# Loading all spectral weights of an attention and Fourier mixing kernel by casting GpSimd DMAs

## The chip, the cores and the metric

The kernel runs on one core of a Trainium2 chip. A core has a matrix engine (PE, with a separate weight load, PEld), a vector engine (DVE), a scalar engine (ACT), GpSimd (POOL) and a queue engine (SP), which work side by side and wait for each other through semaphores. Sixteen DMA engines move data between HBM and the on-chip memory (SBUF). A DMA is issued by an engine's instruction stream, here by SP or by POOL, and it is issued only when the instructions before it in that stream have been issued. PE writes its sums to a second memory, PSUM. The metric is the device time of one execution in microseconds (us); lower is better.

## The reference

Sliding-window attention with a linear distance bias is followed by a mixing layer in the Fourier domain, for 8 sequences of 576 tokens and a width of 512 (8 heads of 64):

```python
def _attn_ref(q, k, v):
    window, scale = 128, 1.0 / np.sqrt(D)
    scores = scale * np.matmul(q, k.transpose(0, 1, 3, 2))
    scores = np.where(mask, scores + bias[None], -1000000000.0)
...
    return np.matmul(attn, v).astype(np.float32)

def _moe_ref(x, w_r, w_i, w_ch):          # 64 modes, each with 512 x 512 matrices w_r and w_i
    X = np.fft.rfft(x, axis=1)
    Xr, Xi = (np.real(X[:, :n_modes]), np.imag(X[:, :n_modes]))
    Yr = np.einsum('bmd,mde->bme', Xr, w_r) - np.einsum('bmd,mde->bme', Xi, w_i)
    Yi = np.einsum('bmd,mde->bme', Xr, w_i) + np.einsum('bmd,mde->bme', Xi, w_r)
    Y[:, :n_modes] = Yr + 1j * Yi
    y = np.fft.irfft(Y, n=S, axis=1)
    u = x + y
    return (u + np.maximum(u @ w_ch, 0.0)).astype(np.float32)
```

All inputs are fp32. Each of the 128 matrices w_r[m] and w_i[m] is 1 MB, and each is used once. The imaginary matrix of mode 0 adds nothing that the output keeps, so the kernel loads 127 of them: 133 MB of the 162.5 MB that it reads.

## The kernel before

**Attention (0 to 138 us).** The work is cut into 16 units of one sequence and four heads. A hand-written table, STAGE, says which step of which unit runs in which stage: scores on PE, exp on ACT, mask and normalisation on DVE, values on PE. SP loads q, k and v in fp32 into the tiles qr, kr and vr. After two units of a sequence PE takes its Fourier transform, and the spectrum goes into the tile XC.

**Weight tiles.** A weight tile holds one matrix, 128 partitions by 4 times 512 elements. `load_w` (L450) issues its load in one of two ways:

- As bf16 (L458 to L460): a GpSimd DMA reads the fp32 matrix and casts it on the way into a tile of 4 KB a partition. During attention one such tile is loaded in each of the stages named in AHEAD, after a small copy on POOL (L533) that waits for a finished piece of x. These 14 tiles make up the pool `early` (EARLY). Seven more go into the `spare` tiles, which are the memory of qr, kr and vr after its last use (LATER). Eight later loads, the list `again` (L545), go into `early` a second time.
- As fp32 (L462 to L466): an SP DMA copies the matrix unchanged into a tile of 8 KB a partition, and the matmul reads every second bf16 half-word of it, `bitcast(BF16)[:, 1::2]`, which is the fp32 number cut to bf16. The pool `wpool` has six such tiles (NWA), `w2` two (NWB). The last matrix is loaded in three parts.

**The stream (138 to 409 us).** The loop over g (L812) takes four modes at a time, and within it the steps i. A step runs the matmuls of one or two weight tiles into the PSUM tile `acc` (L838), four a tile, with XC as the stationary operand. Then it issues one load: from `again` while that list lasts (L847), otherwise a load into the pool of the tile just used (L849), which waits for PE to have read that tile. After the step of the last tile of `again` (K1, L851) the memory of attention's right side is free: the pool `w2` is opened and loaded, the matrix w_ch goes into the tile wch (L861), and POOL prepares FM, FC and pairs (L866 to L877), which the tail uses. From g = 8 on each step also runs one piece of side work from a list (L883): transforms of the first half of the spectrum back to rows Z and ZW, and products of the tokens with w_ch.

**The order of the queues.** Instructions of an engine run in the order of the program. Before L544 POOL has a memset of YT (L541), the tile that collects the mixed spectra.

**The tail (409 to 442 us).** In the last group the partial sums `pa` are taken (`late_end`, L552), and six small DMAs on POOL put rows of them into Z (L557, issued at L616). When the last matrix has come, its rows go the same way on SP and POOL (L918 to L938). Then the output's tiles are finished (`activate`, `finish`), and SP stores them.

Of the kernel before, what the change touches and what calls it, by code (L numbers as in the profile page):

```python
# [10 lines left out]
FP32 = mybir.dt.float32  # L11
BF16 = mybir.dt.bfloat16
# [8 lines left out]
P = 128  # L21
# [378 lines left out]
def kernel(  # L400
# [10 lines left out]
    nc = tc.nc  # L411
    ctx.enter_context(tc.manual_schedule(engines=ALL | {SP}))
    B, H, S, _ = q.shape
    NM, DM, _ = moe_w_r.shape
    AHEAD = {stage: 1 for stage in range(1, 14)}
    LATER = {13: 2, 14: 2, 15: 3}
    EARLY, NWA, NWB, AGAIN = 14, 6, 2, 8
    HM = NM // 2

    const = ctx.enter_context(tc.tile_pool(name="const", bufs=1))  # L420
# [9 lines left out]
    early = actx1.enter_context(  # L430
        tc.tile_pool(name="w1", bufs=EARLY, side="right", reuse_waits="tile")
    )
# [3 lines left out]
    spare = [raw[w][:, i].rearrange("p e j d -> p (e j d)") for w in "qk" for i in range(2)]  # L436
    vflat = raw["v"].rearrange("p u s h d -> p (u s h d)")
    spare += [vflat[:, 2 * DM * i :] for i in range(3)]
    spare = [t[:, : 2 * DM].bitcast(BF16).rearrange("p (a e) -> p a e", a=4) for t in spare]
# [7 lines left out]
    turns[1].remove(1)  # L447
    wq, homes, todo_w, again = {}, {}, [i for turn in turns for i in turn], []

    def load_w(n, pool, bf16, chosen=None):  # L450


        for i in ([i for i in todo_w if i not in again][:n] if chosen is None else chosen):
            todo_w.remove(i)
            src = (moe_w_r, moe_w_i)[i % 2][i // 2].rearrange("(p a) e -> p a e", a=4)
            homes[i] = pool
            if bf16:
                t = spare.pop(0) if pool is None else pool.tile([P, 4, DM], BF16, tag="w", name="w")  # L458
                nc.gpsimd.dma_start(out=t, in_=src)
                wq[i] = [t[:, a] for a in range(4)]  # L460
            else:
                t = pool.tile([P, 4, DM], FP32, tag="w", name="w")  # L462
                for part in ((slice(0, 4),) if i < 2 * NM - 1
                             else (slice(0, 2), slice(2, 3), slice(3, 4))):
                    nc.sync.dma_start(out=t[:, part], in_=src[:, part])
                wq[i] = [t[:, a].bitcast(BF16)[:, 1::2] for a in range(4)]  # L466

    with ExitStack() as actx:
        at = _Attention(tc, actx, q, k, v, (ident, F, FT), x, XC, raw)
        n = len(at.units)  # L470
        for w, u in (("q", 0), ("k", 0), ("q", 1), ("k", 1), ("v", 0), ("v", 1)):
            at.load(w, u)
        done = set()

        def run(name, arg, u):
            if 0 <= u < n and (name, arg, u) not in done:
                done.add((name, arg, u))
                getattr(at, name)(u, arg)

        make_identity(nc, ident)  # L480
        pool = _Scratch(x[:, B - 2 :].rearrange("p b t c -> p (b t c)").bitcast(FP32))
        wt = at.ps.tile([P, P], FP32, tag="av", bufs=1, name="warm")
        for _ in range(24):
            nc.tensor.matmul(wt, lhsT=ident, rhs=ident, start=True, stop=True)
        table = _forward_table(nc, pool, F, S)
        next(table)
        nc.vector.memset(norm, 2.0 / S)
        nc.vector.memset(norm[:32], 1.0 / S)
        for t in at.qkT:
            nc.vector.memset(t[:, 1, :, S:], 0.0)  # L490
        at.distances(pool)
        at.fixtures(0)
        load_w(1, early, True)
        next(table, None)
        at.fixtures(1)
        nc.gpsimd.memset(XC[:, 4 * NC * NM :], 0.0)
        run("cast", "q", 0)
        run("transpose", "q", 0)
        run("cast", "k", 0)
        run("transpose", "k", 0)  # L500
        run("evacuate", "q", 0)
        for h in (1, 3):
            at.decay(h)
        run("evacuate", "k", 0)
        run("score", 1, 0)
        for h in (0, 2, 1, 3):
            at.offset(h)
        run("cast", "q", 1)
        run("transpose", "q", 1)
        run("evacuate", "q", 1)  # L510
        run("score", 0, 0)
        run("exp", 1, 0)
        for h in (0, 2):
            at.decay(h)
        run("exp", 0, 0)
        run("cast", "k", 1)
        run("cast", "v", 0)
        side = {0: [(at.offset, 4), (at.offset, 6), (at.decay, 5), (at.offset, 5), (at.decay, 7),
                    (at.offset, 7), (at.decay, 4), (at.decay, 6)]}
        lags = [lag for _, _, lag in STAGE]  # L520
        for stage in range(min(lags), n + max(lags)):
            for name, arg, lag in STAGE:
                run(name, arg, stage - lag)
                if name in ("transpose", "exp") and side.get(stage):
                    for _ in range(1 + (name == "transpose")):
                        fn, h = side[stage].pop(0)
                        fn(h)
            if stage == 3:
                at.inverse_table()
            if stage in AHEAD:  # L530
                if stage:
                    b, g = at.units[stage - 1]
                    nc.gpsimd.tensor_copy(gate[:1, :1], x[:1, b, 0, 256 * g : 256 * g + 1])  # L533
                load_w(AHEAD[stage], early, True)
            if stage in LATER:
                load_w(LATER[stage], None, True)

    with ExitStack() as mctx:
        fix = mctx.enter_context(tc.tile_pool(name="fix", bufs=1))
# [2 lines left out]
        pool = mctx.enter_context(tc.tile_pool(name="fin", bufs=2))  # L542
        wctx = mctx.enter_context(ExitStack())
        wpool = wctx.enter_context(tc.tile_pool(name="w", bufs=NWA, reuse_waits="tile"))  # L544
        again = todo_w[4 : 4 + 2 * AGAIN : 2]  # L545
        load_w(NWA, wpool, False)
        lctx, pctx = ExitStack(), ExitStack()
        lps = lctx.enter_context(tc.tile_pool(name="lps", bufs=1, side="right", space=PSUM))
        ps = pctx.enter_context(tc.tile_pool(name="fps", bufs=1, space=PSUM))
# [259 lines left out]
        quads, side, recycle = [], [], list(again)  # L809
        ZW = Z = XW = FM = FC = pairs = wch = w2 = None  # L810
        K1 = spot[again[-1]]
        for g in range(NM // 4):  # L812
# [5 lines left out]
            for i in range(8):  # L818
# [25 lines left out]
                own = next((t for t in homes if spot[t] == k), None)  # L844
                if own is None:
                    continue
                if recycle:  # L847
                    load_w(1, early, True, [recycle.pop(0)])
                elif homes[own] not in (early, None):  # L849
                    load_w(1, homes[own], False)  # L850
                if k == K1:  # L851
                    actx1.close()
                    w2 = mctx.enter_context(
                        tc.tile_pool(name="w2", bufs=NWB, side="right", reuse_waits="tile")
                    )
                    load_w(NWB, w2, False)
                    right = mctx.enter_context(
                        tc.tile_pool(name="late", bufs=1, side="right", reuse_waits="tile")
                    )
                    wch = right.tile([P, 4, DM], BF16, name="wch")  # L860
                    nc.gpsimd.dma_start(out=wch, in_=moe_w_ch.rearrange("(a p) e -> p a e", p=P))  # L861
                    ZW = right.tile([P, B // 2, 2, DM], BF16, name="ZW")
                    Z = right.tile([P, B // 2, 2, DM], BF16, name="Z")
                    XW = right.tile([P, len(units), 2, DM], BF16, name="XW")
                    FM = right.tile([P, 2, 2 * P], BF16, name="FM")
                    nc.gpsimd.memset(FM, 0.0)  # L866
                    for b in range(2):
                        nc.gpsimd.dma_start(
                            out=FM.rearrange("(k v) b s -> k v b s", v=16)[:, b, b],
                            in_=FT[64 * b + 56 : 64 * b + 64, b, : 2 * P],  # L870
                        )
                    FC = right.tile([P, P], BF16, name="FC")
                    pairs = right.tile([P, P], BF16, name="pairs")
                    nc.gpsimd.memset(FC, 0.0)
                    for i, rows in enumerate((slice(0, 64), slice(64, P))):
                        nc.gpsimd.tensor_copy(FC[rows, i::2], FT[rows, i, FULL * P :])
                        nc.gpsimd.tensor_copy(pairs[:, i::2], ident[:, rows])  # L877
# [101 lines left out]
```

## Time and profile before

| | |
|---|---|
| Runs | 444.54, 446.43, 444.14 us; median 444.54 |
| Span of the profiled execution | 441.7 us, 8410 instructions |
| PE, PEld, DVE, ACT, POOL busy | 332.8, 179.9, 184.5, 162.1, 50.2 us |
| HBM read, written | 162.53 MB, 9.44 MB |
| DMA queue q1 (issued by SP) | 140.56 MB, 82.2% of sixteen engines' span |
| DMA queue q0 (issued by POOL) | 15.84 MB, 18.1% |
| L838, matmuls with the weights | 93.1 us busy, 498 ns each, 62.3 us idle before them |
| Weight loads on SP, issue to landing | 17.9 us (w_i, x49), 16.0 us (w_r, x48) |
| Weight loads on POOL into `early`, issue to landing | 8.8 us (w_r, x12), 8.3 us (w_i, x10) |

The span is the time from the first to the last instruction; the device time of a run has a few microseconds around it. The bytes of a DMA queue are those that arrive, so that a casting DMA counts 512 KB for a matrix of 1024 KB. The page cuts the span into 40 slices of 11.04 us and gives the busy share of each engine in tenths. L12 is line 12 of the code of the kernel before. "A <- B" among the waits says that A stood idle until B released it.

### The profile page before, as it was taken

What the parts mean: (1) busy time and instruction counts of PE and PEld (TensorE: products, weight loads), DVE (VectorE), ACT (ScalarE), POOL (GpSimd) and SP (SyncE); (2) the same over time, 40 slices, a digit from 0 to 9 for tenths busy, and PEclk for the clock granted to TensorE, in tenths of its full rate; (3) what the DMA queues carried; (4) which work ended last, traced back from release to release, by engine and by line L of the source; (5) the groups of instructions that cost most, each with busy time, mean ns of one, the idle gap of its engine ahead of it and who ended that gap; (6) DMA issues with size and microseconds to landing.
All of it is one profiled execution on the core that took longest, in us unless ns stands there. A gap on an engine that the chain in (4) does not pass through costs nothing. (4 is left out here: it accounts for less than half of the span.)

```text
span 441.7 us, 8410 instructions
## 1 busy us (share of the span) xinstructions
PE 332.8 (75%) x3509; PEld 179.9 (41%) x3509; DVE 184.5 (42%) x332; ACT 162.1 (37%) x211; POOL 50.2 (11%) x107
## 2 busy tenths in 40 slices
PE   5589899879886454454545597999979999879982
PEld 4367677667664221121112133444434444333440
DVE  7789899887863200010000021332222223122694
ACT  6849899978960000000000011232222322101781
POOL 8711010101302200110000000000000000002500
PEclk9969999999998855555555569999999999999998
DMA  8999999999999999999999999999999999997498
GB/s 282 321 325 280 299 322 298 317 294 301 225 214 315 319 316 316 331 383 426 419 422 421 422 422 418 420 421 418 421 419 421 421 418 419 421 422 313 170 376 322
DMA packets 53209, 156.92 MB, mean 355 GB/s; under 512 B 4772, under 2 KB 23860, under 8 KB 40756
## 3 DMA queue, kind: packets, MB, share of 16 engines
q1 hardware_dynamic: 47860, 140.56, 82.2%
q0 software_dynamic: 5312, 15.84, 18.1%
q8 instruction: 27, 0.44, 0.4%
q14 instruction: 10, 0.08, 0.0%
HBM read 162.53 MB, written 9.44 MB: 389 GB/s over the span
## 5 line engine op out<-in xcount | busy, mean ns | idle before, releaser
L838 PE MATMUL acc<-w,XC 128*32 128x512 bf16 x456 | 93.1, 498 | 62.3 <-DMA w<-in_moe_w_r_dram 34.0
L838 PEld LDWEIGHTS <-XC 128*32 128x32 bf16 x508 | 39.4, 149 | 114.5 <-issue 100.1
L294 ACT ACTIVATE att<-sc 128x1024 bf16<-128x1024 f32 x64 | 64.1, 1032 | 10.7 <-PE sc L284 10.6
L604 ACT CAST ZW<-zw 128x512 bf16<-128x512 f32 x8 | 4.7, 585 | 147.6 <-PE zw L602 147.6
L331 PE MATMUL av<-vb,att 128*128 128x132 bf16 (+1 forms) x576 | 38.6, 218 | 10.9 <-DVE x L347 5.9
L331 PEld LDWEIGHTS <-att 128*128 128x128 bf16 x704 | 36.7, 99 | 16.3 <-DVE x L347 10.2
L576 DVE TENSOR_SCALAR yq<-acc 128x512 bf16<-128x512 f32 x14 | 9.6, 686 | 79.6 <-PE acc L838 79.6
L670 PE MATMUL my<-wch,xT 128*64 128x512 bf16 x288 | 34.5, 381 | 5.8 <-ACT x L701 4.3
L679 ACT CAST XW<-my 128x512 bf16<-128x512 f32 x36 | 19.3, 589 | 51.0 <-PE my L627 51.0
L651 DVE COPY xT<-tr 128x1024 bf16<-128x1024 bf16 x18 | 12.4, 691 | 55.0 <-PE tr L649 55.0
L256 ACT COPY qkT<-tp 128x1152 bf16<-128x1152 bf16 x30 | 33.5, 1116 | 2.8 <-PE tp L250 2.1
L616 POOL DMA_DIRECT2D Z<-yq x11 | 5.5, 511 | 217.4 <-issue 216.2
L347 DVE TENSOR_TENSOR x<-av,rec 128x640 bf16<-128x640 f32 x32 | 26.4, 824 | 1.1
L284 PE MATMUL sc<-qkT 64*64 64x256 bf16 (+2 forms) x640 | 25.1, 263 | 2.1 <-ACT qkT L256 1.2
L670 PEld LDWEIGHTS <-xT 128*64 128x64 bf16 x288 | 17.2, 109 | 21.7 <-issue 9.3
L794 DVE TENSOR_TENSOR o<-yy,r 128x1024 f32<-128x1024 f32 (+1 forms) x22 | 21.5, 1024 | 4.3 <-ACT r L770 3.2
L233 DVE CAST vb<-vr 64x1024 bf16<-64x1024 f32 x32 | 22.6, 708 | 0.2
L701 ACT CAST x<-my 128x512 bf16<-128x512 f32 x18 | 10.5, 585 | 33.0 <-PE my L627 33.0
L284 PEld LDWEIGHTS <-qkT 64*64 64x64 bf16 x640 | 14.5, 109 | 19.4 <-issue 16.3
L702 DVE CAST x<-my 128x512 bf16<-128x512 f32 x18 | 12.4, 691 | 23.4 <-PE my L627 23.4
L271 PE MATMUL sc<-bias,ident 128*128 128x512 bf16 x64 | 20.8, 409 | 1.3 <-ACT att L294 1.3
L305 DVE TENSOR_TENSOR att<-att,mask 128x1024 bf16<-128x1024 bf16 x32 | 20.6, 683 | 0.0
(130 smaller groups left out, 396.6 us busy)
## 6 DMA issues: line engine op xcount, KB each, us to landing
w<-in_moe_w_i_dram SPq DMA_DIRECT2D x49, 1024.0 KB, 17.9
w<-in_moe_w_r_dram SPq DMA_DIRECT2D x48, 1024.0 KB, 16.0
qr<-in_q_dram SPq DMA_DIRECT2D x16, 576.0 KB, 10.3
kr<-in_k_dram SPq DMA_DIRECT2D x16, 576.0 KB, 8.6
vr<-in_v_dram SPq DMA_DIRECT2D x64, 128.0 KB, 7.6
out_dram<-o SPq DMA_DIRECT2D x13, 512.0 KB, 4.5
w<-in_moe_w_r_dram POOLq DMA_DIRECT2D x12, 512.0 KB, 8.8
w<-in_moe_w_i_dram POOLq DMA_DIRECT2D x10, 512.0 KB, 8.3
```

The lines of the kernel that those rows point to most:

```text
L233: nc.vector.tensor_copy(self.vb[u % 2][row, :, :, :, W * half : W * half + D], src[row, :2])
L256: (self.nc.vector.tensor_copy if u < 2 and w == "q" else self.nc.scalar.copy)(dst.rearrange("q h (p j) -> q h p j", j=TPP), tp.rearrange(" ...
L271: nc.tensor.matmul(sc[:, e], lhsT=self.ident, rhs=self.bias[:, hv].rearrange("p j n -> p (j n)"), start=True, stop=False, skip_group_check ...
L284: nc.tensor.matmul(sc[64 * half : 64 * half + 64, e, j * 256 + c0 : j * 256 + c0 + n], lhsT=qkT[row, 1, h, k0 + j : k0 + P : 2], rhs=qkT[r ...
L294: self.nc.scalar.activation(self.att[u % 2][:, kt * 8 * P : (kt + 1) * 8 * P], sc.rearrange("p e n -> p (e n)"), AF.Exp, scale=1.0 / math. ...
L305: nc.vector.tensor_tensor(out=rows, in0=rows, in1=self.table[:, heads], op=ALU.mult)
L331: nc.tensor.matmul(bank[:, qt * W : qt * W + rhs[j].shape[1]], lhsT=att[:, o : o + P], rhs=rhs[j], start=(n == 0 and j == 0), stop=(n == l ...
L347: nc.vector.tensor_tensor(out=self.x[:, b, :, cs].rearrange("p t (h d) -> p h t d", h=2), in0=tiles[:, :, :, :D], in1=rec.unsqueeze(-1).br ...
L670: nc.tensor.matmul(mm[ROWS[half]], lhsT=lhsT, rhs=wch[:, dt], start=(dt == 0), stop=False, skip_group_check=True,)
L679: nc.scalar.copy(XW[:, j, n], mms[n])
L794: nc.vector.tensor_tensor(out=o[:, c], in0=yy[:, c], in1=r[:, c], op=ALU.add)
L838: nc.tensor.matmul(into[32 * (m % 4) : 32 * (m % 4) + 32], lhsT=XC[:, c0 : c0 + 31 * NM + 1 : NM], rhs=wq[t][a], start=(ri == 0 and a == 0 ...
```

## The change

Every weight tile is loaded by a GpSimd DMA that casts to bf16; the branch that loads fp32 tiles by SP is gone, with its half-word view. The pools keep their memory and hold twice as many tiles of half the size: `wpool` twelve and `w2` four. The list `again` becomes the eight matrices that follow the first twelve. The last matrix still comes in three parts. Lines behind the function move up by six.

```diff
@@ -414,7 +414,7 @@
-    EARLY, NWA, NWB, AGAIN = 14, 6, 2, 8
+    EARLY, NWA, NWB, AGAIN = 14, 12, 4, 8
@@ -447,23 +447,17 @@
-    def load_w(n, pool, bf16, chosen=None):
-
+    def load_w(n, pool, chosen=None):
 
         for i in ([i for i in todo_w if i not in again][:n] if chosen is None else chosen):
             todo_w.remove(i)
             src = (moe_w_r, moe_w_i)[i % 2][i // 2].rearrange("(p a) e -> p a e", a=4)
             homes[i] = pool
-            if bf16:
-                t = spare.pop(0) if pool is None else pool.tile([P, 4, DM], BF16, tag="w", name="w")
-                nc.gpsimd.dma_start(out=t, in_=src)
-                wq[i] = [t[:, a] for a in range(4)]
-            else:
-                t = pool.tile([P, 4, DM], FP32, tag="w", name="w")
-                for part in ((slice(0, 4),) if i < 2 * NM - 1
-                             else (slice(0, 2), slice(2, 3), slice(3, 4))):
-                    nc.sync.dma_start(out=t[:, part], in_=src[:, part])
-                wq[i] = [t[:, a].bitcast(BF16)[:, 1::2] for a in range(4)]
+            t = spare.pop(0) if pool is None else pool.tile([P, 4, DM], BF16, tag="w", name="w")
+            for part in ((slice(0, 4),) if i < 2 * NM - 1
+                         else (slice(0, 2), slice(2, 3), slice(3, 4))):
+                nc.gpsimd.dma_start(out=t[:, part], in_=src[:, part])
+            wq[i] = [t[:, a] for a in range(4)]
@@ -542,8 +536,8 @@
         wpool = wctx.enter_context(tc.tile_pool(name="w", bufs=NWA, reuse_waits="tile"))
-        again = todo_w[4 : 4 + 2 * AGAIN : 2]
-        load_w(NWA, wpool, False)
+        again = todo_w[NWA : NWA + AGAIN]
+        load_w(NWA, wpool)
@@ -845,15 +839,15 @@
                 if recycle:
-                    load_w(1, early, True, [recycle.pop(0)])
+                    load_w(1, early, [recycle.pop(0)])
                 elif homes[own] not in (early, None):
-                    load_w(1, homes[own], False)
+                    load_w(1, homes[own])
                 if k == K1:
                     actx1.close()
                     w2 = mctx.enter_context(
                         tc.tile_pool(name="w2", bufs=NWB, side="right", reuse_waits="tile")
                     )
-                    load_w(NWB, w2, False)
+                    load_w(NWB, w2)
```

The three other calls of `load_w` only lose the argument that chose the type.

More of the change, by code (lines that the diff above doesn't have):

```diff
@@ L492 @@
         at.fixtures(0)
-        load_w(1, early, True)
+        load_w(1, early)
         next(table, None)
@@ L533 @@
                     nc.gpsimd.tensor_copy(gate[:1, :1], x[:1, b, 0, 256 * g : 256 * g + 1])
-                load_w(AHEAD[stage], early, True)
+                load_w(AHEAD[stage], early)
             if stage in LATER:
-                load_w(LATER[stage], None, True)
+                load_w(LATER[stage], None)
     with ExitStack() as mctx:
```

## The prediction

> **What bounds the kernel now.** I read the forty slices of the page first, then the stretches of the stream, then the waits, then single DMAs, and last the chain of waits.
>
> ```profile
> PEclk9969999999998855555555569999999999999998
> DMA  8999999999999999999999999999999999997498
> GB/s 282 321 325 280 299 322 298 317 294 301 225 214 315 319 316 316 331 383 426 419 422 421 422 422 418 420 421 418 421 419 421 421 418 419 421 422 313 170 376 322
> ```
>
> The DMA row stands at 9 from slice 2 to slice 36, 11 us to 408 us: the DMA engines are the bound until the last weight tile, whatever the compute engines do. The GB/s row counts what lands, so a tile cast from 1 MB of fp32 to 0.5 MB of bf16 counts half. Slices 11 and 12 (225, 214) are the only ones in which nearly all traffic is casts.
>
> The next view has the busy time of each engine by stretch: length, busy and (count) of PE, PEld, DVE, ACT, POOL, then the granted clock, the DMA share and GB/s. A share over 1 means that packets overlap on an engine.
>
> ```profile
> 122.20:132.20 10.00, 8.31 (x153) 6.25 (x151) 6.79 (x13) 7.43 (x9) 1.05 (x2) 1.00 1.06 214
> ...
> 210.00:240.00 30.00, 15.95 (x57) 5.35 (x58) 1.99 (x10) 0.00 (x0) 0.00 (x0) 0.50 1.01 421
> 240.00:270.00 30.00, 20.38 (x96) 7.92 (x97) 4.77 (x10) 2.34 (x4) 0.00 (x0) 0.64 1.01 421
> ...
> 330.00:360.00 30.00, 28.50 (x238) 12.63 (x236) 9.11 (x16) 8.29 (x15) 0.00 (x0) 1.00 1.01 420
> 360.00:390.00 30.00, 24.84 (x179) 10.77 (x176) 6.62 (x11) 6.15 (x11) 0.00 (x0) 1.00 1.01 421
> ```
>
> The first row is casts alone, the others plain fp32 tiles alone. Casts land 214 GB/s and so read 428; plain tiles read 421. A tile of 1.0486 MB takes 2.45 us as a cast and 2.49 us plain. PE is busy 28.5 of 30 us at 330 to 360, so it is near a bound of its own there.
>
> The waits, in total, with times and longest:
>
> ```profile
> PE acc L838 <- DMA w<-in_moe_w_r_dram: 34.0, 22, 4.6
> PE acc L838 <- DMA w<-in_moe_w_i_dram: 26.5, 19, 3.0
> POOL wch L861 <- DMA w<-in_moe_w_i_dram: 4.5, 1, 4.5
> ...
> SPq L465 <- PE acc L838: 184.8, 48, 9.7
> ```
>
> PE waits 60.5 us for weights. SP waits 184.8 us for PE to release a tile, but at a DMA share of 1.01 that costs nothing.
>
> Single DMAs of the last attention stages, whose issues on POOL began at 116.25, 116.77, 117.29 and 117.81 us, and the last part of the last tile, issued on SP at 393.1 us; the last number is us from issue to landing:
>
> ```profile
> w<-in_moe_w_i_dram POOLq DMA_DIRECT2D x1, 512.0 KB, 6.0
> qr<-in_moe_w_i_dram POOLq DMA_DIRECT2D x1, 512.0 KB, 7.9
> qr<-in_moe_w_r_dram POOLq DMA_DIRECT2D x1, 512.0 KB, 9.8
> kr<-in_moe_w_r_dram POOLq DMA_DIRECT2D x1, 512.0 KB, 11.8
> w<-in_moe_w_i_dram SPq DMA_DIRECT2D x1, 256.0 KB, 15.2
> ```
>
> The casts land at 122.25, 124.67, 127.09 and 129.61: (129.61 - 122.25) / 3 = 2.45 us each, the pace of the first row above by another route. The stream ends at 393.1 + 15.2 = 408.3. The chain of waits then begins:
>
> ```profile
> 409.38 0.05 issue
> 409.43 0.22 PE tr L914 x2
> ...
> 412.30 1.74 DMA ZW<-F
> ```
>
> It holds the 33.4 us from 408.3 to the end at 441.7, with no weight load in it. So the time is the stream's end plus a fixed tail.
>
> **The change part by part.** *The transfers.* 98 tiles (100 DMAs, the last tile in three) move from SP to POOL and are cast on the way. The bytes read stay the same, and what counts is the pace. By 132.2 us 18 of the 127 tiles have landed (the fifth cast of that row, 118.33 + 13.9). Left are 109 tiles and the 1 MB of wch, 110 units. Before they took (408.3 - 132.2) / 110 = 2.51 us each: 0.02 more than the 2.49 of the stretches, since the sixteen engines don't finish together and the mixed start has short dips. After, the lower bound is the casts' own 2.45; the upper one for this mechanism is the plain 2.49. I take 2.47: the casts' row is the operation itself, and I add the same 0.02. The stream then ends at 132.2 + 110 x 2.47 = 403.9, which is 4.4 us earlier (6.6 at 2.45, 2.2 at 2.49).
>
> *Issue.* Each cast occupies POOL for about 0.53 us (median; 0.757 at most, for wch). 98 x 0.53 = 52 us, against the 2.47 us that a tile has: hidden by seven other tiles in flight. Were that cover gone, each issue would cost about 0.53 us plus the 1.6 us that a 2 KB row of Z needs to land (the page's DMA issues), so the cover matters, but it has some 17 us.
>
> *Sixteen tiles for eight.* The built program makes each POOL DMA wait for the landing of the eighth POOL DMA before it; wch at L861 shows such a wait, 4.5 us. So eight are in flight, as many as now, and the doubled tiles only let PE lag further. I cost this at nothing either way. With eight in flight the queue holds 8 x 2.47 = 20 us of work.
>
> *Queues that are passed.* Three things now share POOL with the loads. First, the memset of YT (L541) stands ahead of the first twelve loads; its 7.4 us wait for attention's last normalisation ends at 135.39, and the loads follow at 135.84. Before, SP issued the first fp32 tile at 129.30 and the rest from 134.7. The cover is three casts into vr still queued: at 2.45 us each they last from 132.2 to 139.5 by landing, and some 1.3 us less, to 138.2, on the first of the sixteen engines (the spread of a cast's semaphore counts). The new loads deliver from 135.84 + 1.6 = 137.4. No hole, with 0.8 us to spare; each us of delay beyond that costs one us, and I keep 0 to 2. Second, FM's memset (L866), which waited 33.6 us for PE, now has loads behind it; but wch, before it, must wait for a tile eleven later than the one PE must release, so it is reached when PE has long passed. Wch lands about 132.2 + 40 x 2.47 = 231 rather than at 197.6; its first reader (L602) runs at 255.9. Third, the six Z rows of L557 wait for the landings of the last weights. They now come behind these in one ring, and are read in the tail only from the units of batch rows 2 and up; their own sources come at 404.9. I cost both at nothing; if Z's cover fails it is 1 to 2 us.
>
> *PE.* The moving operand becomes dense bf16 instead of every second half-word. At full clock the fp32 tiles of the last group took 387 ns a matmul (x24), the bf16 ones in kr, qr and vr 386 to 399: nothing. To end 4.4 us earlier PE must give up idle time; of that gain some 2.4 us arises after 255 us, and PE's waits for weights after 255 sum to 8.6 us, 3.0 of them at 383 to 388, behind its tightest stretch. PE can follow.
>
> The Trainium skill, page "SBUF — State Buffer", section "SBUF: two separate sides", speaks against the change: a DMA issued from GpSimd needs descriptors that GpSimd can't write while VectorE holds the shared port, and it names 620 ns growing to about 3100 ns. The trace's row does not agree: issues of L459 average 562 ns (12 into w from w_r) and reach 747 ns with DVE 75 to 94% busy. By the page, if every issue met such an operation, POOL's 3.1 us per tile would replace 2.47, an estimate of 110 x 0.6 = 66 us more; by the row, nothing.
>
> The sum: 441.7 - 4.4 = 437.3 us of span. The median of the runs is 444.54, 2.8 us over the span; that I leave as it is. 444.54 - 4.4 = **440.1 us**.
>
> **The rivals.** *Casts pace no better than plain tiles.* For: only four landings carry the 2.45, and mixed slices (316 landed, so 421 read) show plain pace. Against: 214 holds over ten us by a second count. At 2.51 the stream ends where it did; with a hole of 0 to 2 us, 444.5 to 446.5.
>
> *Packets lose their overlap: slower.* From the stretches, a cast's packet takes 1.06 x 160 us / (2140 KB / 4096 B = 522) = 325 ns, a plain one 1.01 x 480 us / (12630 KB / 8192 B = 1542) = 314. Casts win only because packets overlap 6%. If a hundred tiles from one ring overlap like plain ones (1.01), a tile takes 8 x 325 / 1.01 = 2.57, with the 0.02 2.59, and the stream ends at 417.1: 453.3 us. It decides for slower from a share below 1.036 (2.51 + 0.02 = 2.53 a tile). For it: ten us is short. Against: those ten us are this very queue, alone, with DVE and ACT busier than later.
>
> *PE takes over as the bound.* At 343 to 354 two tiles with their side work take 5.37 us, against 4.94 for two casts. If PE could regain nothing after 337, where the lead is (337 - 132) x 0.016 = 3.3 us, the result is 441.3. Against: the 5.4 us of waits from 337 on.
>
> **How the numbers follow.** The forecast has 0.55 (its own range, 2.45 to 2.49: 437.9 to 442.3), casts at plain pace 0.24, lost overlap 0.17, PE 0.04. A measurement of this kernel tells 0.5%, 2.2 us, from no change. Faster: 0.55 and 0.03 of the PE case, less 0.02 at the edge, 0.56; slower: 0.17 and 0.02 for a hole atop plain pace, 0.19; same: 0.25. The range, 437.0 to 448.0, leaves out most of the lost overlap and 0.04 below.
>
> **What would show it.** Right: 212 to 215 GB/s at a DMA share near 1.06 from 150 to 390 us, the last weight landing near 404, and a tail of 33 us. Wrong: a share near 1.01 with about 204 GB/s (lost overlap), 210 (plain pace), a dip at 136 to 140 (the hole), POOL issues well over 0.6 us, or PE without waits for weights from 330 on.

## The result, and the profile after

The changed kernel takes 442.2 us in the median of 20 runs, against 445.23 us for the kernel before in the same comparison. The ratio is 0.9934, with a 95% interval of 0.9919 to 0.9949: faster by 0.66%, 2.9 us. The forecast was faster by 4.4 us. The direction and the mechanism were right, and the forecast gain was half as large again as what came.

The profiled execution spans 439.1 us, 2.6 us less than the one before. Its slices, with the granted clock, the DMA engines' busy share and what they landed:

```profile
span 439.1 us, 8379 instructions
...
PEclk9979899999899965555555569999999999989997
DMA  8999999999999999999999999999999999998598
GB/s 285 321 333 294 311 285 304 308 295 305 229 214 193 213 213 214 213 214 213 214 211 215 213 214 213 213 213 213 215 213 213 214 212 214 214 214 156 200 369 304
```

The DMA row is still full up to the last weights, so the bound hasn't moved. From slice 14 to slice 36 the GB/s row stands at 211 to 215, mostly 213 or 214, where it stood at about 420 with plain tiles alone. A cast lands half of what it reads, so 213 to 214 is 426 to 428 read, and the stream reads 1.2 to 1.7% more a second than the 421 of before. One slice drops out: 193, at 132 to 143 us.

By stretch (length, busy time and count of PE, PEld, DVE, ACT and POOL, then granted clock, DMA share, GB/s):

```profile
135.00:138.00 3.00, 1.82 (x30) 1.50 (x27) 1.73 (x4) 0.00 (x0) 1.31 (x3) 1.00 1.01 203
138.00:141.00 3.00, 1.50 (x18) 1.27 (x20) 0.62 (x2) 0.55 (x2) 3.00 (x7) 1.00 0.88 152
140.00:145.00 5.00, 4.16 (x62) 3.15 (x62) 1.38 (x5) 0.00 (x0) 1.90 (x4) 1.00 1.05 206
210.00:240.00 30.00, 15.42 (x56) 5.05 (x53) 1.94 (x9) 0.00 (x0) 9.54 (x21) 0.50 1.08 213
330.00:360.00 30.00, 28.57 (x246) 12.98 (x242) 9.11 (x16) 8.29 (x15) 6.34 (x12) 1.00 1.06 213
```

The share of 1.06 that ten microseconds showed before now holds through the stream, also at 330 to 360, where PE is busy 28.6 of 30 us. At 138 to 141 the DMA engines ran short: 152 GB/s at a share of 0.88. The same stretch of the kernel before had no such dip:

```profile
138.00:141.00 3.00, 2.72 (x17) 1.44 (x20) 0.02 (x1) 0.00 (x0) 0.70 (x2) 0.59 1.03 317
```

POOL's instructions around that place in the changed kernel (start, length, what, and the idle time before them):

```profile
128.12 1.05 POOL L459 DMA_DIRECT2D vr<-in_moe_w_r_dram  x2 [5.66 <-DVE vb L233]
136.60 0.45 POOL L535 MEMSET YT<- 128x256 bf16 x1 [7.43 <-DVE x L347]
137.14 1.06 POOL L459 DMA_DIRECT2D w<-in_moe_w_i_dram  x2
138.18 1.07 POOL L459 DMA_DIRECT2D w<-in_moe_w_r_dram  x2
```

The memset ended its wait at 136.60, where the prediction had 135.39, and the first load of the stream was issued at 137.14 instead of 135.84. That is the hole that the prediction weighed.

The waits with the new queue in them, and the issues by duration (min/median/max, ns):

```profile
POOL w L459 <- DMA w<-in_moe_w_r_dram: 80.8, 42, 2.8
POOL w L459 <- DMA w<-in_moe_w_i_dram: 60.9, 32, 2.3
...
PE acc L832 <- DMA w<-in_moe_w_i_dram: 29.9, 22, 2.6
PE acc L832 <- DMA w<-in_moe_w_r_dram: 29.2, 23, 1.9
```

```profile
L459 POOL DMA_DIRECT2D w<-in_moe_w_i_dram x62: 527/527/575, 35.0 to 390.4; - x62
L459 POOL DMA_DIRECT2D w<-in_moe_w_r_dram x60: 527/527/747, 11.4 to 383.3; - x60
```

POOL now mostly waits for the landing of an earlier DMA (141.7 us), which is the limit of eight in flight: 96 of its 101 weight issues after 141 us come within 0.7 us of the landing of the eighth DMA before them. It hardly waits for PE to release a tile. PE waits 59.1 us for weights, 1.4 us less than before. The last part of the last tile was issued at 390.43:

```profile
w<-in_moe_w_i_dram POOLq DMA_DIRECT2D x1, 128.0 KB, 14.6
```

It landed at 405.0, against 408.3 before: 3.3 us earlier. The rest of the way to the end, 34.1 us, is 0.7 us longer than before. The chain shows that all of it arises from the output's stores on (start, length, what):

```profile
406.09 0.05 issue
...
408.99 1.78 DMA ZW<-F
...
425.36 0.34 SPq L790
...
425.79 5.74 DMA out_dram<-o
```

In the kernel before, the store of that chain was:

```profile
428.93 5.45 DMA out_dram<-o
```

The pieces up to 425.36 stand where they stood before in relation to the last weight, to a few hundredths of a microsecond. Then SP issues the long store 0.14 us later, the store takes 5.74 us instead of 5.45, and 0.24 us more come after it.

### The profile page after: what moved, and what is told of

Read it like the earlier page. It is cut to its first block, busy times and chain, and to the rows that moved or that the text cites. A ratio compares the mean times of both kernels' runs of the same rounds, so it can differ in the third digit from the quotient of the medians.

```text
span 439.1 us, 8379 instructions
## 1 busy us (share of the span) xinstructions
PE 328.8 (75%) x3488; PEld 180.7 (41%) x3509; DVE 184.4 (42%) x332; ACT 162.1 (37%) x211; POOL 103.7 (24%) x207
## 5 line engine op out<-in xcount | busy, mean ns | idle before, releaser
L832 PE MATMUL acc<-w,XC 128*32 128x512 bf16 x456 | 91.2, 475 | 60.8 <-DMA w<-in_moe_w_i_dram 29.9
L459 POOL DMA_DIRECT2D w<-in_moe_w_i_dram x62 | 32.8, 530 | 99.3 <-DMA w<-in_moe_w_i_dram 59.0
L459 POOL DMA_DIRECT2D w<-in_moe_w_r_dram x60 | 32.0, 535 | 89.9 <-DMA w<-in_moe_w_r_dram 71.7
L527 POOL COPY gate<-x 1x1 bf16<-1x1 bf16 x13 | 6.3, 487 | 83.7 <-DVE x L347 83.7
```

What stands on the lines that cost most here:

```text
L459: nc.gpsimd.dma_start(out=t[:, part], in_=src[:, part])
L832: nc.tensor.matmul(into[32 * (m % 4) : 32 * (m % 4) + 32], lhsT=XC[:, c0 : c0 + 31 * NM + 1 : NM], rhs=wq[t][a], start=(ri == 0 and a == 0 ...
```

## The experiments

Four kernels shared one chip and its runs of the kernel before; two more shared another such session.

**Cast or queue.** The kernel before, with its fp32 tiles, but all loads issued by GpSimd:

```diff
-                    nc.sync.dma_start(out=t[:, part], in_=src[:, part])
+                    nc.gpsimd.dma_start(out=t[:, part], in_=src[:, part])
```

> The kernel before, with its fp32 weight tiles (eight, unchanged 8 KB) issued by GpSimd instead of SP and not cast. Theory 'cast': the better pace of the changed kernel belongs to the cast. Then plain tiles from this queue keep the plain pace, 2.49 us a tile, DMA share near 1.01 and 420 to 421 GB/s from 210 to 390 us, and the memset of YT ahead of the loads costs up to 1 us: ratio 1.000 to 1.004. Rival 'queue': the pace belongs to the queue that GpSimd feeds. Then 427 GB/s, 2.46 us a tile and a ratio near the changed kernel's 0.993.

Measured: 445.6 us against 444.57, ratio 1.0018, interval 1.0004 to 1.0032. The stretches of that kernel:

```profile
210.00:240.00 30.00, 14.55 (x54) 5.20 (x55) 1.94 (x9) 0.00 (x0) 6.31 (x12) 0.50 1.02 422
...
330.00:360.00 30.00, 28.34 (x235) 12.47 (x233) 9.12 (x16) 8.16 (x16) 6.31 (x12) 1.00 1.01 421
360.00:390.00 30.00, 24.98 (x189) 11.24 (x189) 6.63 (x11) 6.96 (x13) 6.31 (x12) 1.00 1.01 420
```

Plain tiles keep the plain pace on GpSimd's queue, 420 to 422 GB/s at a share of 1.01 to 1.02. The rival "queue" falls: the better pace needs the cast. Whether it is the conversion itself or only that half as many bytes are written, no run tells. The move to POOL by itself costs about 0.8 us (0.0018 x 444.6), within the range of the first theory. That the memset's wait is the reason is not shown: this profile has a share of 1.05 at 138 to 141 us, although the wait ended only at 136.77, and the first tile of the stream landed 3.03 us after the tile before, some 0.5 us late.

**Number of tiles.** The changed kernel with eight tiles in the pools instead of sixteen:

```diff
-    EARLY, NWA, NWB, AGAIN = 14, 12, 4, 8
+    EARLY, NWA, NWB, AGAIN = 14, 6, 2, 8
```

> The changed kernel with six and two weight tiles in the pools, as many as before, instead of twelve and four. Theory 'cast': eight DMAs are in flight either way, so 213 to 214 GB/s from 150 to 390 us and a ratio of 0.992 to 0.996 as for the changed kernel. Rival 'depth': the gain came from PE being allowed to lag further; then waits of POOL for PE open gaps at 330 to 362 us, GB/s there falls below 211, and the ratio is 0.998 to 1.002.

Measured: 442.41 us against 444.57, ratio 0.9953, interval 0.9933 to 0.9974, which overlaps the changed kernel's. Two of its stretches, and the largest of POOL's waits:

```profile
330.00:360.00 30.00, 28.21 (x240) 12.65 (x238) 9.12 (x16) 8.30 (x15) 6.36 (x12) 1.00 1.06 213
360.00:390.00 30.00, 24.82 (x179) 11.15 (x176) 6.45 (x12) 5.57 (x10) 6.88 (x13) 1.00 1.06 214
```

```profile
POOL w L459 <- PE acc L832: 143.5, 39, 8.3
```

With eight tiles POOL waits 143.5 us for PE instead of for landings, and the DMA engines don't notice: 213 to 214 GB/s in PE's tightest stretch too. The doubled number of tiles isn't what made the kernel faster. A share of 0.1% or 0.2% for it can't be excluded by these intervals.

**The cover taken away.** The same with four tiles:

```diff
-    EARLY, NWA, NWB, AGAIN = 14, 12, 4, 8
+    EARLY, NWA, NWB, AGAIN = 14, 3, 1, 8
```

> The changed kernel with three and one weight tiles in the pools. This takes away the cover of the issue: a load waits for PE to have read the tile four before it, PE holds two tiles at a time and takes 5.4 us for two with their side work, and four tiles are 9.8 us of DMA work. Theory 'cover': DMA engines run empty where PE is slow, above all at 250 to 262 us (half clock) and 330 to 362 us, GB/s there below 205, ratio 1.005 to 1.05. If the depth of the queue doesn't matter at all (a load is always issued in time), the ratio stays near 0.993.

Measured: 470.52 us against 444.57, ratio 1.059, interval 1.0567 to 1.0614. That is slower than the range expected, which ended at 1.05.

```profile
210.00:240.00 30.00, 13.88 (x50) 4.71 (x50) 2.01 (x6) 0.00 (x0) 5.27 (x10) 0.50 1.05 197
240.00:270.00 30.00, 16.05 (x68) 5.86 (x64) 3.17 (x11) 0.58 (x1) 6.09 (x12) 0.57 1.00 182
...
330.00:360.00 30.00, 25.75 (x200) 11.75 (x198) 8.43 (x15) 7.21 (x13) 5.68 (x11) 0.94 0.99 183
```

```profile
POOL w L459 <- PE acc L832: 200.6, 46, 8.1
```

The loss isn't confined to where PE is near its bound: at 210 to 240 us PE is busy less than half the time, and still 197 GB/s land instead of 213. By the landings in the trace, 89 of the 106 weight issues after 141 us found one to three other DMAs in flight. In the changed kernel 98 of 101 found seven, and with eight tiles 102 of 103 found five to seven, at the full rate. So the cover that the prediction named was needed, and taking it away cost 28 us (470.52 against 442.41 with eight tiles on the same chip). That the uncovered time is POOL's issue and a DMA's way to its first bytes, as the prediction had it, fits this but was not measured by itself.

**The hole.** The changed kernel with the memset of YT on DVE, so that no load waits behind it:

```diff
-        nc.gpsimd.memset(YT[:, 1, :, :, HM - 4 :], 0.0)
+        nc.vector.memset(YT[:, 1, :, :, HM - 4 :], 0.0)
```

> The changed kernel with the memset of YT on DVE, so that the first twelve loads no longer stand behind its wait on POOL. If the dip at 138 to 140 us (127 GB/s, DMA share 0.79) comes from that wait, it goes: share 1.05 from 135 to 145 us, the last weight lands 1.0 us earlier, ratio 0.9905 to 0.992. If the dip has another cause (the memory of attention coming free late) or the end doesn't follow the stream's start, the ratio stays at 0.993 to 0.994.

Measured: 440.0 us against 444.57, ratio 0.9916, interval 0.9896 to 0.9936. The stretch of the hole and POOL's first loads of the stream:

```profile
135.00:138.00 3.00, 1.46 (x20) 1.24 (x20) 1.15 (x4) 0.55 (x2) 2.33 (x5) 1.00 1.06 213
138.00:141.00 3.00, 2.72 (x17) 1.34 (x20) 0.17 (x2) 0.00 (x0) 1.06 (x2) 0.54 1.06 212
140.00:145.00 5.00, 4.16 (x54) 2.53 (x53) 1.38 (x5) 0.00 (x0) 1.06 (x2) 0.84 1.07 214
```

```profile
129.76 0.53 POOL L459 DMA_DIRECT2D w<-in_moe_w_i_dram  x1 [1.82 <-PE sc L284]
134.68 0.53 POOL L459 DMA_DIRECT2D w<-in_moe_w_i_dram  x1 [4.39 <-issue]
```

The dip is gone, and the first two loads go out 7.4 and 3.0 us earlier; 1.2 us of this comes from attention, which ran earlier in this execution (the last casts into vr went out at 126.88 instead of 128.12). Two intervals from different sessions overlap, so both kernels were set side by side.

> The changed kernel once more, beside the next run on the same chip. Theory 'cast': 213 to 214 GB/s in the stream, a dip at 137 to 141 us of about 1 us, ratio 0.992 to 0.996. If the dip hangs on where attention happens to end (136.6 us for the last normalisation there, 135.4 in the profile of before), its size differs from the first profile's.

> The changed kernel with the memset of YT on DVE, again, to set it against the changed kernel on one chip. Theory 'hole': no dip from 135 to 145 us, and 0.5 to 1.2 us below the run before it in the median, ratio 0.990 to 0.993. If the hole is worth nothing, both medians agree within 0.3 us.

Measured: the changed kernel 442.28 us, ratio 0.9937 (0.9916 to 0.9957); with the memset on DVE 441.0 us, ratio 0.9908 (0.9891 to 0.9925). The medians differ by 1.3 us, somewhat more than expected, in the same direction as in the first session. In this profile of the changed kernel the normalisation ended at 135.89, and the dip was smaller:

```profile
138.00:141.00 3.00, 2.12 (x26) 1.75 (x30) 0.53 (x2) 0.00 (x0) 2.13 (x5) 1.00 0.95 178
```

The share was 0.88 after a wait that ended at 136.60, and 0.95 after one that ended at 135.89. But the size of the dip doesn't follow the end of attention alone: with eight tiles the wait ended at 135.92, and the first tile of the stream still landed 3.76 us after the tile before, 1.3 us late.

What the profiles don't show is the earlier end of the stream that was expected. In the first pair the last weight landed at 404.3 us with the memset on DVE, against 405.0, and attention had run 1.2 us earlier. In the second it landed at 405.8 against 405.7, and attention had run 0.7 us later (128.09 instead of 127.39 for those casts into vr). So the stretches show that the dip goes, and the runs that the kernel gains; that the whole 1.3 us is the dip is not shown. The version with the memset on DVE was the fastest of all that ran, by 1.3 us over the changed kernel on the same chip; the intervals of the two ratios overlap.

## Why the prediction was right, and where its size was off

*The bound.* That the DMA engines' stream sets the time, and the tail follows it, held, with a tail 0.7 us longer than before: the DMA row stands at 9 up to slice 36, 395 us, the share is 1.06 up to 400 us, and the last weight came 3.3 us earlier. (The prediction read its own row a little too far: slice 36 ended at 397.5 us there, and slice 37, up to 408.6, stands at 7.)

*The pace.* The prediction took 2.47 us a tile from casts at 2.45 and 0.02 for unevenness. The trace's semaphore counts put the last engine's landing of the 3rd tile of the stream at 147.97 and of the last whole tile but one at 399.97 us; between them lie 102 units, with two small copies of FM among them: 252.0 / 102 = 2.47. This term was right, and the first experiment shows that it belongs to the cast.

*The hole.* This is the step that failed: "No hole, with 0.8 us to spare". The queue order was read rightly, and the range kept 0 to 2 us for it, but the sum took 0. In the profiled execution the landing of the first tile of the stream came 3.46 us after the tile before, where others take 2.46: 1.0 us lost. The stream's end, forecast at 403.9, came at 405.0. In part this is the late memset: the loads went out 1.3 us later than counted on (137.14 against 135.84), which by the prediction's own rule, with 0.8 us to spare, costs 0.5. The moment moves between executions (135.39, 135.89, 136.60 for the same instruction), and a cover of that size was counted as whole.

The rest is the cover itself, which was counted too long. In the second profile of the changed kernel the loads went out 0.6 us later than forecast, and the last cast ahead of them landed at 140.88, 1.4 us later than the forecast's 139.5. That should have left 1.6 us to spare; the first tile still landed 2.88 us after that cast, 0.4 us late. One term that was too small is the spread among the sixteen engines: taken as 1.3 us, it was 1.5 and 2.1 us at that cast in the two profiles. What else the cover lacked stays open.

*The tail.* Forecast at 33.4 us, it took 34.1. The chain shows the stores, not the six Z rows behind the last weights, which were costed at nothing: up to the stores every piece keeps its place to a few hundredths of a microsecond. Whether the 0.7 us belong to the change stays open: the six other profiles of changed kernels, the one with plain tiles among them, had tails of 33.7 to 34.4 us, and the kernel before has one profile alone.

*The sum.* In the profiled spans 2.6 us came of the 4.4: the stream ended 1.1 us later than forecast, of which the hole is 1.0, and the tail was 0.7 longer. The runs say 2.9, so 1.5 us are missing. With the memset on DVE the ratios are 0.9916 and 0.9908, which is 3.7 and 4.1 us: without the wait ahead of the loads most of the forecast gain is there. The start of the sum moves too: the 18th tile, 132.2 us in the prediction and in the first profile after, landed at 133.6 in the second.

*Issue on POOL, and eight in flight.* Right: 527 ns in the median, 747 at most, and no trace of it in the DMA rate. The Trainium skill, page "SBUF — State Buffer", section "SBUF: two separate sides", says that descriptor writing on GpSimd is blocked while VectorE holds the shared port. The 66 us that the prediction estimated from it did not come: 122 issues into `w` never took more than 747 ns. The longest issue of any run took 940 ns, so none was blocked for the length the page names; whether VectorE held the port in that way at all, the trace doesn't tell.

*The rivals.* "Packets lose their overlap" is out by the share of 1.06 over 240 us. "Casts pace no better" is out by the rate, though what spoke for it, the mixed slices at plain pace, was real: there the pair has the plain pace, and why was not tried. "PE takes over": PE had no wait for weights at all from 328 to 365 us, as that rival asks, but it took up the lead behind that stretch, where such waits remained (3.8 us from 365 to 400 us).

## What to carry to other kernels

Where DMA engines are the bound, compare the pace of the two kinds of transfer in stretches where each runs alone, with their share of busy time beside it, and check it by landings: ten microseconds of an old profile gave the new stream's pace to 1%. When loads move to another engine's queue, list what stands ahead of them there and waits; here a small memset cost about 1 us (1.0 and 0.4 us in two profiles, 1.3 us in the runs) out of a gain of 4. And when the cover is less than the time by which that wait moves between executions, don't count it as whole. A deeper pool pays only as far as it keeps enough transfers in flight: here sixteen tiles gave nothing measurable over eight, and four cost 28 us.

## What the runs showed of the hardware

- A casting DMA from fp32 to bf16 reads 1.2 to 1.7% more a second than a plain one (426 to 428 against 421 GB/s), although each of its packets takes longer (about 325 against 314 ns): they overlap more, share 1.06 against 1.01. This wasn't a matter of the issuing engine. Why they overlap more was not tried.
- When casts and plain tiles share the engines half and half (150 to 180 us of the kernel before), the pair lands 316 GB/s, which is 421 read: the mixture has the plain pace, and nothing of the cast's.
- The sixteen engines drift apart in the stream, by amounts that differ between executions of one kernel. In the first profile of the changed kernel most tiles' semaphore counts come within 1.2 to 1.4 us of each other from 142 to 318 us, and within 2.4 us at the end; in the second it was mostly 1.9 to 2.1 up to 300 us, and 3.1 at the end. In the kernel before it was 1.7 to 2.1 with plain tiles from 188 to 312 us, and 3.4 at the end. Several of the steps fall together with a 16 KB fetch of instructions, others don't; the cause was not tried.
